# Four accumulators that were halves of two-bank tiles become one-bank tiles, with a new order list

## The chip, the cores and the metric

The kernel runs on one core of one Trainium2 chip. The metric is the device time of one execution in microseconds (us). The engines are TensorE (PE, with its weight loads as PEld), VectorE (DVE), ScalarE (ACT), GpSimd (POOL) and SyncE (SP, which issues DMAs).

## What is computed

Attention with a soft cap, then a gated feed-forward block with a token mix, then a second block that ends in a square product. Cut to what matters:

```python
s = cap * tanh(q @ k.T / 8 / cap)                       # 4 batches, 12 heads, 448 tokens, 64 each
x = softmax(s) @ v                                      # to (4, 448, 768)
h = relu(x @ w_in); u, v = halves of h                  # 1024 columns
x = (u * (w_spatial @ layer_norm(v) + b_spatial)) @ w_out
theta = x @ w_theta
y = w_tok_r @ (x * cos(theta)) + w_tok_i @ (x * sin(theta))
u = x + y
out = u + relu(u @ w_ch)                                # (4, 448, 768) @ (768, 768): the last stage
```

## The kernel before

All data are fp32. TensorE multiplies in fp32r, and for fp32's precision each factor is split in a high part and a low part (a cast, then `difference` L407, the rest as fp32r), so that each term is three products (`three`, `products`, whose matmuls all bear line L404).

The program is a plan. Functions such as `run`, `copy_out`, `plus` and `finish` don't issue instructions but record operations, each with an engine, keys that it reads and writes, and a function that issues it. A table of numbers, `ORDER` (lines 47 to about 330), lists the operations of the whole kernel, some 3430, in the order in which they are issued; `Plan.run` goes through it. The plan asserts only that no operation stands ahead of one whose keys it needs. Each engine then runs its own instructions in that order, and waits between engines follow from the tiles that instructions read and write: an instruction that touches a tile waits for the earlier ones on other engines which touch the same tile, unless both only read.

The last stage computes `u @ w_ch` for two pairs of batches with seven sums of block products in place of eight (`pair(c0, t)`). `a` and `S` are the weights and sums of them (`split_a` L1989, S on L2001, L2006 and L2010), `x` the split activations (cast L2065, difference L407, sums t_f on L2097). A `run` adds nine matmuls, 128 rows by 448 columns each, into one PSUM bank: three pieces of the inner dimension by three products. The pieces of several runs are interleaved on TensorE. When a bank is full it is read by one of `copy_out` (ACT, L2148, `p<-f_ps`) or `plus` (DVE, L2152, `p<-f_ps,p`); from the sums p, `finish` makes the result (DVE L2162), turns it round by four transposes into another bank (PE L2172, `o_ps`), copies it (ACT) and stores it (SP). The last piece of each pair ends in `end_of` (L2207 to L2234).

Six banks serve in turn (`new_bank` over `BANKS`, line 1892 on). Two are tiles of one bank in the pool `ps_mm`. The other four are the halves, 512 columns each, of two tiles of 1024 columns in the pool `ps_s`, which before that held the attention's scores and the transposes `x_ps`. `open_bank` makes such a tile, `bank_of` cuts out the half:

```python
fin["s", k] = ps_s.tile([128, 1024], F32, tag="s", name="f_ps")
...
return (fin["mm"][key[1]] if key[0] == "mm" else fin["s", key[1]][:, 512 * key[2]:512 * key[2] + 512])[:, 0:S]
```

The plan has a key for each half, `("s", k, h)`; the tile is one.

Of the kernel before, what the change touches and what calls it, by code (L numbers as in the profile page):

```python
# [342 lines left out]
def attn_moe_moe2_kernel(ctx: ExitStack, tc: tile.TileContext, q, k, v, cap, w_in, w_sp, b_sp, w_out,  # L343
# [13 lines left out]
    plan = Plan()  # L357
# [1531 lines left out]
    def open_bank(k):  # L1889
        fin["s", k] = ps_s.tile([128, 1024], F32, tag="s", name="f_ps")  # L1890
# [9 lines left out]
    def bank_of(key):  # L1900
        return (fin["mm"][key[1]] if key[0] == "mm" else fin["s", key[1]][:, 512 * key[2]:512 * key[2] + 512])[:, 0:S]
# [449 lines left out]
```

## Time and profile before

| | |
|---|---|
| time, three runs | 762.16, 763.88, 765.02 us (median 763.88) |
| profiled execution | 763.6 us, of which the span from first to last instruction 761.8 |
| mean granted TensorE clock | 0.997 of full speed |
| busy in the span: PE, DVE, ACT, POOL | 743.9, 620.2, 476.0, 343.0 us |
| share of the chain that ended last: PE, DVE, ACT, POOL | 72, 5, 2, 1% |

A busy time is the sum of the instructions of an engine. The stages follow one another with some overlap: attention and the first block to about 460 us, theta and the token mix to about 668, the last stage from there (its first products from about 650 on). For a stage the question is what TensorE's next instruction waits for, which the waits, the chain and the timeline tell; for a matmul the start counts, since the next begins before the end that the profile models.

### The profile page before, as it was taken

How to read it: one execution, taken by the hardware profiler on the slowest of the kernel's cores; microseconds unless marked ns; L12 is line 12 of the kernel's file. 1: busy time of each engine (PE TensorE's matmuls, PEld its weight loads, DVE VectorE, ACT ScalarE, POOL GpSimd, SP SyncE). 2: the span in 40 equal slices, each digit the busy share in tenths (PEclk: the TensorE clock that was granted, in tenths of full speed). 3: DMA queues.
4: the chain of work that ended last, by engine and by line, in shares of the span. 5: the costliest groups of instructions: out<-in, count | busy, mean ns of one | idle time of the engine just before them, and what ended most of it. 6: DMA issues, size and time to landing. Idle time of an engine off the chain costs nothing.

```text
span 761.8 us, 11555 instructions
## 1 busy us (share of the span) xinstructions
PE 743.9 (98%) x3965; PEld 643.1 (84%) x3965; DVE 620.2 (81%) x992; ACT 476.0 (62%) x798; POOL 343.0 (45%) x464
## 2 busy tenths in 40 slices
PE   7999999999999999999999999999999999999997
PEld 4655678888888888887899999999999999888896
DVE  4969988798687978799987776899878877997865
ACT  4989878788779878896454644543514533553453
POOL 4889675544555465561100012232332422877650
PEclk9999999999999999999999999999999999999999
DMA  6677333242432541431343330011210000000135
GB/s 174 190 202 182 109 101 93 57 106 64 101 93 51 123 98 33 119 76 43 92 144 115 121 94 1 1 43 43 62 42 22 22 2 1 1 0 1 37 108 147
DMA packets 82062, 59.31 MB, mean 78 GB/s; under 512 B 47330, under 2 KB 75204, under 8 KB 82004
## 3 DMA queue, kind: packets, MB, share of 16 engines
q1 hardware_dynamic: 80100, 54.61, 27.1%
q0 software_dynamic: 1152, 3.64, 1.5%
q8 instruction: 31, 0.51, 0.3%
q10 hardware_dynamic: 752, 0.33, 0.2%
q14 instruction: 27, 0.22, 0.1%
HBM read 44.18 MB, written 5.62 MB: 65 GB/s over the span
## 4 chain that ended last, share of the span: by engine, by line
PE 72%; DVE 5%; ACT 2%; POOL 1%; issue 1%; DVEq 0%; POOLq 0%; ACTq 0%
PE ps_mm L404 16%; PE y_ps L404 12%; PE th_ps L404 12%; PE f_ps L404 10%; PE acc L404 7%; PE sc L404 5%; PE ps_sum L404 3%; PE ps_av L404 3%; PE o_ps L2172 1%; PE tqk L711 1%; PE x_ps L1624 1%; DVE ll L407 1%; DVE p L2152 1%; DVE s L995 1%; PE tok_ps L1500 1%
## 5 line engine op out<-in xcount | busy, mean ns | idle before, releaser
L404 PE MATMUL y_ps<-tok_h,zt 128*128 128x448 f32 x312 | 99.0, 368 | 0.1
L824 ACT ACTIVATE e<-e,cap_sb 128x896 f32<-128x896 f32 x72 | 74.8, 1043 | 1.0
L821 ACT ACTIVATE e<-sc,icap 128x896 f32<-128x896 f32 x72 | 72.1, 1005 | 4.7 <-PE sc L404 3.8
L407 DVE TENSOR_TENSOR ll<-e,hh 128x896 fp32r<-128x896 f32 x54 | 59.3, 1103 | 16.0 <-ACT hh L829 14.1
L404 PEld LDWEIGHTS y_ps<-tok_h,zt 128*128 128x128 f32 x312 | 58.6, 188 | 5.1 <-POOL zt L407 0.4
L404 PE MATMUL th_ps<-th_ah,x 128*128 128x256 f32 x288 | 57.4, 284 | 0.0
L404 PE MATMUL y_ps<-tok_l,zt 128*128 128x448 f32 x156 | 57.4, 368 | 0.0
L407 POOL TENSOR_TENSOR zt<-z,zt 128x1024 fp32r<-128x1024 f32 x12 | 29.6, 2470 | 59.2 <-ACT zt L1739 59.2
L407 POOL TENSOR_TENSOR x<-x,x 128x384 fp32r<-128x384 f32 (+1 forms) x15 | 18.5, 1242 | 74.0 <-ACT x L1565 65.1
L404 PE MATMUL f_ps<-x,S 128*128 128x448 f32 x216 | 49.8, 372 | 1.6 <-DVE p L2152 1.0
L1678 POOL TENSOR_SCALAR n<-n 128x512 f32<-128x512 f32 (+1 forms) x24 | 16.0, 669 | 76.8 <-DVE n L1675 76.8
L404 PE MATMUL ps_mm<-w_in_h,x 128*128 128x512 f32 (+1 forms) x132 | 47.8, 400 | 0.9 <-DVE gated L1256 0.8
L404 PE MATMUL ps_mm<-x,w_in_h 128*128 128x448 f32 x168 | 48.3, 368 | 0.0
L404 PEld LDWEIGHTS th_ps<-th_ah,x 128*128 128x128 f32 x288 | 46.8, 190 | 0.8
L404 PE MATMUL sc<-yl,XH 128*128 128x448 f32 x126 | 46.4, 368 | 0.0
L404 PEld LDWEIGHTS f_ps<-x,S 128*128 128x128 f32 x216 | 39.6, 188 | 6.3 <-DVE p L2152 1.6
L404 PE MATMUL f_ps<-x,a 128*128 128x448 f32 (+2 forms) x171 | 38.8, 362 | 2.3 <-DVE p L2152 1.7
L404 PE MATMUL acc<-ll,vh 128*128 128x448 f32 x108 | 40.1, 371 | 0.8 <-DVE ll L407 0.8
L1739 ACT CAST zt<-z 128x1024 fp32r<-128x1024 f32 (+2 forms) x36 | 24.3, 691 | 26.2 <-DVE z L1710 22.7
L404 PE MATMUL th_ps<-th_al,x 128*128 128x256 f32 x144 | 40.6, 282 | 0.0
L450 ACT ACTIVATE hb<-bits 128x384 f32<-128x384 f32 (+4 forms) x40 | 22.7, 567 | 27.6 <-DMA bits<-in_moe_w_ch_dram 15.5
L404 PE MATMUL acc<-hh,vh 128*128 128x448 f32 x108 | 39.6, 367 | 0.0
(328 smaller groups left out, 2366.1 us busy)
## 6 DMA issues: line engine op xcount, KB each, us to landing
y<-y SPq DMA_DIRECT2D x60, 112.0 KB, 2.2
bits<-in_moe_w_ch_dram SPq DMA_DIRECT2D x12, 384.0 KB, 3.1
out_dram<-o SPq DMA_DIRECT2D x23, 192.0 KB, 2.4
rq<-in_q_dram SPq DMA_DIRECT2D x33, 128.0 KB, 2.7
rk<-in_k_dram SPq DMA_DIRECT2D x11, 384.0 KB
r<-d SPq DMA_DIRECT2D x16, 224.0 KB, 3.8
rv<-in_v_dram SPq DMA_DIRECT2D x18, 192.0 KB, 2.6
w_in_bits<-in_moe_w_in_dram POOLq DMA_DIRECT2D x6, 512.0 KB, 4.6
```

The source lines that it names most:

```text
L404: nc.tensor.matmul(out=ps, lhsT=a, rhs=r, start=(first and i == 0), stop=(last and i == len(terms) - 1))
L407: (engine or nc.vector).tensor_tensor(out=o, in0=x, in1=f32(hi), op=ALU.subtract)
L450: nc.scalar.activation(out=hb(), in_=f32(words()[:, :, 1]), func=ACTF.Copy, scale=2.0 ** -112)
L711: nc.tensor.transpose(o, a, ident)
L821: nc.scalar.activation(out=st["e", g], in_=src, func=ACTF.Tanh, scale=icap)
L824: nc.scalar.activation(out=st["e", g], in_=st["e", g], func=ACTF.Exp, scale=cap_sb)
L995: nc.vector.reciprocal(out=st["s"], in_=st["s"])
L1500: nc.tensor.transpose(o, a[:, kk * 128:(kk + 1) * 128], ident[0:n, 0:n])
L1624: nc.tensor.transpose(o, x2(b, m)[:, p * 128:p * 128 + 128], ident)
L1678: nc.gpsimd.tensor_scalar(out=sd["n"], in0=sd["n"], scalar1=1.0, scalar2=-MAGIC, op0=ALU.mult, op1=ALU.add)
L1739: nc.scalar.copy(out=o, in_=a)
L2152: op("dve", t + 0.2, 0.54, lambda: TT(out=fin["p", o], in0=bank_of(kb), in1=fin["p", j], op=ALU.add), r=[kb, ("p", j)], w=[("p", o)])
```

## The change

The pool `ps_s` goes to the right side of PSUM and gets a stack of its own, which one new operation `open_banks` closes when the last stage opens; in its place the operation opens the pool `ps_f` with four tiles of one bank each. `bank_of` takes these tiles. That is one operation less than before, and `ORDER` is another list over the whole kernel. Each engine has the same instructions in the same numbers; line numbers after the first edit move by 1, and by 3 from the last stage on (L2148 becomes L2151, L2152 becomes L2155).

```diff
 ORDER = [
-    9, 10, 38, 4, 7, 8, 12, 5, 36, 0, 6, 11, 35, 2, 31, 33, 37, 13, 14, 15, 29, 17, 16, 24, 30, 27, 32, 23, 18, 22, 34,
...
-    ps_s = Slots(plan, ctx.enter_context(tc.tile_pool(name="ps_s", bufs=1, space=PSUM)), 2)
     ps_1 = ctx.enter_context(tc.tile_pool(name="ps_1", bufs=1, space=PSUM))
     ps_mm = Slots(plan, ctx.enter_context(tc.tile_pool(name="ps_mm", bufs=1, space=PSUM)), 2)
+    ps_stack = ctx.enter_context(ExitStack())
+    ps_s = Slots(plan, ps_stack.enter_context(tc.tile_pool(name="ps_s", bufs=1, space=PSUM, side="right")), 2)
...
-    def open_bank(k):
-        fin["s", k] = ps_s.tile([128, 1024], F32, tag="s", name="f_ps")
+    def open_banks():
+        ps_stack.close()
+        ps_f = ctx.enter_context(tc.tile_pool(name="ps_f", bufs=1, space=PSUM, side="right", reuse_waits="tile"))
+        for k in range(2):
+            for h in range(2):
+                fin["s", k, h] = ps_f.tile([128, 512], F32, tag="f%d%d" % (k, h), name="f_ps")
 
     op("none", t - 4.0, 0.0, open_mm, w=[("mm", 0), ("mm", 1)])
     BANKS = [("mm", 0), ("mm", 1)]
-    for _ in range(2):
-        sk = ring("s", 2)[1]
-        halves = [("s", sk, h) for h in range(2)]
-        op("none", t0 - 2.0, 0.0, lambda sk=sk: open_bank(sk), w=[("s", sk)] + halves)
-        BANKS += halves
+    for sk in range(2):
+        BANKS += [("s", sk, h) for h in range(2)]
+    op("none", t0 - 2.0, 0.0, open_banks, w=[("s", 0), ("s", 1)] + BANKS[2:])
 
     def bank_of(key):
-        return (fin["mm"][key[1]] if key[0] == "mm" else fin["s", key[1]][:, 512 * key[2]:512 * key[2] + 512])[:, 0:S]
+        return (fin["mm"][key[1]] if key[0] == "mm" else fin[key])[:, 0:S]
```

In the rows of the order, a row is an instruction (or as many alike as `x3` says), with its line, what it writes and reads, and the engines whose semaphores it waits on. Before, `f_ps_7044` and `f_ps_7192` are the two tiles of two banks, `f_ps_7050` and `f_ps_7051` those of `ps_mm`. TensorE at the start of the last stage, at about 667.7 to 671.5 us of the trace of before:

```order
L404 MATMUL f_ps_7192<-x_6997,a_7138 128x448 [waits PE_49,Activation_49]
L404 MATMUL f_ps_7192<-x_6997,a_7138 128x448
L404 MATMUL f_ps_7192<-x_6997,a_7138 128x448 [waits DVE_49]
L404 MATMUL f_ps_7044<-x_6997,a_7138 128x448 x3
L404 MATMUL f_ps_7044<-x_7042,a_7152 128x448 [waits Activation_49]
L404 MATMUL f_ps_7044<-x_7042,a_7152 128x448
L404 MATMUL f_ps_7044<-x_7042,a_7152 128x448 [waits Pool_49]
L404 MATMUL f_ps_7192<-x_6997,a_7138 128x448 x3
```

The three products into `f_ps_7044` of row 4 go into its second half; row 5 goes on in that same half and waits for ScalarE, which reads the first half. After, the tiles of one bank are `f_ps_7096` to `f_ps_7099`, those of `ps_mm` are `f_ps_7076` and `f_ps_7077`. The same place on TensorE:

```order
L405 MATMUL f_ps_7099<-x_6997,a_7127 128x448 [waits PE_49]
L405 MATMUL f_ps_7099<-x_6997,a_7127 128x448 x2
L405 MATMUL f_ps_7098<-x_6997,a_7127 128x448 x3
L405 MATMUL f_ps_7098<-x_7044,a_7143 128x448 [waits Activation_49]
L405 MATMUL f_ps_7098<-x_7044,a_7143 128x448
L405 MATMUL f_ps_7098<-x_7044,a_7143 128x448 [waits Pool_49]
L405 MATMUL f_ps_7097<-x_7044,a_7143 128x448 x3
L405 MATMUL f_ps_7098<-x_7010,a_7081 128x448 x2
L405 MATMUL f_ps_7098<-x_7010,a_7081 128x448 [waits DVE_49]
```

The wait for ScalarE in row 4 is now one for an operand, as ScalarE's read is of `f_ps_7096` and no row here touches that. The second place is TensorE before at about 697.5 to 703 us, with two stops, at 699.65 (row 4) and 701.85 (row 8):

```order
L404 MATMUL f_ps_7192<-x_7042,a_7225 128x448 [waits DVE_49]
L404 MATMUL f_ps_7192<-x_7042,a_7225 128x448 x2
L404 MATMUL f_ps_7192<-x_7010,a_7225 128x448 x3
L404 MATMUL f_ps_7192<-x_7164,a_7405 128x448 [waits DVE_49]
L404 MATMUL f_ps_7192<-x_7164,a_7405 128x448 x2
L404 MATMUL f_ps_7192<-x_7169,S_6979 128x448 x2
L404 MATMUL f_ps_7192<-x_7169,S_6985 128x448
L404 MATMUL f_ps_7192<-x_7204,S_6982 128x448 [waits DVE_49]
L404 MATMUL f_ps_7192<-x_7204,S_6982 128x448
```

All rows are of one tile, of which VectorE reads one half while TensorE writes the other. The same place after:

```order
L405 MATMUL f_ps_7098<-x_7044,a_7237 128x448 [waits DVE_49]
L405 MATMUL f_ps_7098<-x_7044,a_7237 128x448 x2
L405 MATMUL f_ps_7098<-x_7010,a_7237 128x448 x3
L405 MATMUL f_ps_7099<-x_7216,S_6979 128x448 [waits DVE_49]
L405 MATMUL f_ps_7099<-x_7216,S_6979 128x448
L405 MATMUL f_ps_7099<-x_7216,S_6985 128x448
L405 MATMUL f_ps_7098<-x_7168,a_7410 128x448 x3
L405 MATMUL f_ps_7099<-x_7213,S_6982 128x448 x2
```

Two tiles take turns here, and a wait for VectorE stands only ahead of a bank's first product.

## Rows read from the trace of the kernel before

**Rows 1.** The page: busy time of each engine, share of span, instructions.

```profile
PE 743.9 (98%) x3965; PEld 643.1 (84%) x3965; DVE 620.2 (81%) x992; ACT 476.0 (62%) x798; POOL 343.0 (45%) x464
```

**Rows 2.** By stage: window, us, busy of PE, PEld, DVE, ACT, POOL; clock, DMA, GB/s.

```profile
460.00:640.00 180.00, 180.00 (x1219) 171.77 (x1219) 148.39 (x282) 77.35 (x150) 54.81 (x44) 1.00 0.09 25
...
664.00:690.00 26.00, 24.76 (x119) 21.92 (x118) 23.61 (x29) 12.53 (x28) 20.68 (x16) 1.00 0.00 0
690.00:720.00 30.00, 27.85 (x138) 24.35 (x137) 24.02 (x38) 12.52 (x30) 19.58 (x15) 1.00 0.09 24
720.00:750.00 30.00, 29.88 (x175) 26.82 (x173) 20.99 (x31) 14.52 (x40) 14.03 (x11) 1.00 0.40 107
```

**Rows 3.** Chain of waits from 664 us on: start us, us, what.

```profile
669.14 0.02 issue
669.16 0.54 ACT p L2148
669.70 0.04 issue
669.75 11.41 PE f_ps L404 x54
...
698.97 0.64 DVE p L2152
```

**Rows 4.** Waits of TensorE, 640 to 762 us: for what; total, times, longest.

```profile
PE f_ps L404 <- DVE p L2152: 2.7, 5, 0.7
PE f_ps L404 <- ACT p L2148: 1.2, 2, 0.6
PE o_ps L2222 <- DVE x L2209: 0.6, 2, 0.3
```

**Rows 5.** Timeline of TensorE: start us, us, instruction, count [idle before, releaser].

```profile
667.73 1.40 PE L404 MATMUL f_ps<-x,a 128*128 128x448 f32 x6
669.75 1.49 PE L404 MATMUL f_ps<-x,a 128*128 128x448 f32 x6 [0.62 <-ACT p L2148]
...
697.46 1.48 PE L404 MATMUL f_ps<-x,a 128*128 128x448 f32 x6
699.65 0.88 PE L404 MATMUL f_ps<-x,a 128*128 128x448 f32 x3 [0.72 <-DVE p L2152]
...
720.25 4.11 PE L404 MATMUL f_ps<-x,S 128*128 128x448 f32 x18
...
750.16 1.49 PE L404 MATMUL f_ps<-x,S 128*128 128x448 f32 x6 [0.28 <-DVE p L2152]
...
754.81 0.97 PE L404 MATMUL f_ps<-x,a 128*128 128x256 f32 x6 [0.28 <-DVE p L2152]
```

**Rows 6.** Groups of the page: busy us, mean ns, then idle before.

```profile
L404 PE MATMUL f_ps<-x,S 128*128 128x448 f32 x216 | 49.8, 372 | 1.6 <-DVE p L2152 1.0
```

**Rows 7.** Waits of TensorE's weight loads, 640 to 762 us.

```profile
PEld f_ps L404 <- DVE p L2152: 4.6, 6, 1.1
PEld f_ps L404 <- ACT p L2148: 2.4, 3, 1.0
...
PEld y_ps L404 <- POOL zt L407: 0.4, 1, 0.4
```

**Rows 8.** Timeline of VectorE in the same stretch.

```profile
649.98 0.61 DVE L407 TENSOR_TENSOR x<-x,x 128x448 fp32r<-128x448 f32 x1
...
659.63 0.41 DVE L1710 TENSOR_TENSOR z<-z,x_ps 128x256 f32<-128x256 f32 x1
...
680.21 1.57 DVE L407 TENSOR_TENSOR x<-t_f,x 128x448 fp32r<-128x448 f32 x1
...
698.97 1.16 DVE L2152 TENSOR_TENSOR p<-f_ps,p 128x448 f32<-128x448 f32 x2 [0.96 <-PE f_ps L404]
...
754.13 0.62 DVE L2152 TENSOR_TENSOR p<-f_ps,p 128x448 f32<-128x448 f32 x1 [1.47 <-PE f_ps L404]
```

**Rows 9.** Waits of TensorE, 60 to 340 and 340 to 640 us: the largest of each.

```profile
PE w_sp_ps L1096 <- DVE w_sp_l L407: 1.1, 2, 0.6
...
PE ps_mm L404 <- DVE gated L1256: 0.8, 1, 0.8
```

**Rows 10.** By stage again: the ten us after the w_sp waits.

```profile
80.00:90.00 10.00, 9.38 (x35) 7.54 (x36) 9.71 (x14) 7.76 (x12) 5.58 (x7) 0.83 0.43 129
```

341 rows, old and new, of the table ORDER are left out of this document.

## The prediction

> **What bounds the kernel now.** I read the page first: TensorE is busy in 743.9 of 761.8 us, the next engine, VectorE, in 620.2 [rows 1]. So the end can only move by what TensorE stands still, and the whole kernel holds less than 20 us of that. Then the busy time by stage [rows 2]: in 460 to 640 us TensorE has no gap (180.00 of 180.00), in the last stage it has: 24.76 of 26.00, 27.85 of 30.00, 29.88 of 30.00. The reader is to see beside it that VectorE stands at 23.61 of 26.00 us in the first of these stretches, nearly full too; that comes back as a rival.
>
> What the gaps are is told by the chain of waits [rows 3]. It goes matmul, then a read of 0.54 to 0.64 us on ScalarE or VectorE, then matmul. At 669.16 the copy L2148 begins 0.02 us after the matmuls before it, and the matmuls go on 0.05 us after it ends: both engines stand waiting for each other, with nothing queued between. The order of the kernel before shows why: PE writes three products into a bank, ACT or DVE reads the other half of the same two-bank tile, and PE goes on with the fourth product into the same bank as before. The reader waits for TensorE's three, which it does not read, and TensorE waits for the reader, whose half it does not write. Both are tied by the tile's name alone.
>
> TensorE's waits from 640 us on [rows 4] are all of this sort but the last two at the very end: DVE p five times, 2.7 us, ACT p twice, 1.2 us. The timeline of TensorE shows them one by one [rows 5]: 669.75, 699.65, 750.16 and 754.81 stand there; 681.76 (0.62), 701.85 (0.72) and 712.12 (0.71) read like the first two. Two more leave no gap in the row but stretch it: 697.46 and one inside the run that begins at 720.25. That makes nine.
>
> **The change, part by part.** *The stops.* A matmul's row lasts 0.37 us (mean 372 ns, [rows 6]) but the next one begins sooner: six take 1.40 us at 667.73 [rows 5], so the pitch is (1.40 - 0.37) / 5 = 0.206 us. The idle time of a row counts from the end of the 0.37, so each gap hides a further 0.37 - 0.21 = 0.16 us; and the six after a stop take 1.49 instead of 1.40, another 0.09. Seven stops with a gap: 2.7 + 1.2 = 3.9 us of idle time [rows 4], 7 x 0.16 = 1.1, 7 x 0.09 = 0.6, together 5.6 us. The stop at 697.46 adds some 0.2 (1.48 for six, and a start 0.14 late), the one in the run at 720.25 as much (4.11 us for 18, where 17 x 0.206 + 0.37 makes 3.87). Sum: **6.0 us**, all of it on TensorE, which the chain follows. By the idle column alone it would be 3.9.
>
> Idle and loss part here because matmuls overlap. The Trainium skill (Perfetto Trace Analysis, Identifying the Most-Contended Engine) says that matmul busy time is a bad measure, since pipelined matmuls look otherwise in the trace than they cost; it names the share of weight loads as the better one. The weight loads' waits for the same readers are 4.6 + 2.4 = 7.0 us [rows 7]; the sum by these would give 763.6 - 7.0 + 0.5 = 757.1, by the idle column 760.2. I keep the sum by starts.
>
> *Does the edit remove all nine?* In the kernel after each bank is a tile, so a read waits for the writes of its own bank. What is left is true reuse: by the order of after at least 15 matmuls (15 x 0.206 = 3.1 us) stand between the last product into a bank and the first of its next use, where before five stops had none at all. The read in between takes 0.64 us [rows 3]. It has 2.4 us to spare, more than any one instruction of VectorE that I saw in its way (1.57 us, [rows 8]). So these waits go to nothing, at most to a few tenths if two slow VectorE instructions fall together.
>
> *What is late next.* TensorE then asks earlier for its operands, by up to 6 us at the end. They are splits on VectorE and GpSimd (L407) and the pieces S. The same 128x448 split takes 0.61 us at 649.98 and 1.57 at 680.21, with GpSimd busy beside it [rows 8], so one operand can come 0.96 us later than another of its kind. Before, such waits appear only under other matmuls, 0.4 us for zt [rows 7]. Bounds: 0 where the new order keeps the distance, 1.0 where one slow split is met on the path. I take **0.5 us**, in the middle, since 0.4 is the only such row. At the end of the stage the gain passes on: VectorE waits 1.47 us for TensorE at 754.13 [rows 8], so nothing of the tail stands on VectorE.
>
> *Closing the pool and opening a new one* issues no instruction: counts on every engine are the same. But the new pool's tiles take the place of the old one's, so their first writes wait until those were read. The last user of these tiles is x_ps, transposes that VectorE reads for the last time at 659.63 [rows 8]; the first product into that place comes at 667.73 [rows 5], 7.7 us after the read ends, and the other tile was free before. The new order brings x_ps 12 matmuls earlier, which widens this. Price nothing; if the cover were gone, one wait of at most the read's 0.41 us.
>
> *The rest of the order.* The list was made anew over the whole kernel, so all engines' rows shift by a few places, with the same operations and durations. From 460 to 640 us there is nothing to win [rows 2]. From 60 to 460 us TensorE's waits are few and short: w_sp 1.1 us, gated 0.8 [rows 9], nine groups and 4.6 us in all to 640 us. A new order can take half of these away or breed as many. There is a costlier kind of row: after the two w_sp waits of 79.08 and 80.39 the granted clock is 0.83 in the ten us from 80 on [rows 10], at 1.2 GHz for part of it, where 0.17 x 10 = 1.7 us of full-speed time is missing. If that stretch is met once more or once less the time moves by about 2.5. I take **0**, with -2.5 to +2.5 as bounds.
>
> Sum against the profiled execution: 763.6 - 6.0 + 0.5 + 0 = **758.1 us**, 0.7% less. The profiled execution lies 0.3 us under the median of 763.88, so no correction is made.
>
> **The rivals.** *A: the stop goes, the next engine is late.* For it: VectorE is busy in 23.61 of 26.00 us from 664 to 690 [rows 2]; without the two stops there (1.7 us) that stretch would be 24.3 us, and VectorE 97% full, with no room for an order that is not perfect. Against: it falls to 24.02 of 30.00 in the next stretch, and part of its time is waiting for the very same stops (0.96 us at 698.97, [rows 8]). Price: the 1.7 us are not won, and three slow splits more at 0.96 are met, 2.9: 763.6 - 6.0 + 1.7 + 2.9 = 762.2 us.
>
> *B: slower, by waits in the attention stage.* The new order starts late there one more operand of TensorE at several places, as w_sp now, and after each the clock falls: 1.1 us of waiting [rows 9] and 1.7 us of clock [rows 10] are 2.8 us a place. Two places leave 758.1 + 5.6 = 763.7, so from there on it decides; three make 766.5, four 769.3. For it: from 60 to 90 us VectorE is full, so an operand moved back a place is late by its whole duration. Against: only one such place exists in 400 us of the present order, and the moves are of a few rows.
>
> *C: the stops stay.* There are six banks before and six after, and if the banks were too few the wait would only take another name. The Trainium skill (Perfetto Trace Analysis, Optimization Strategy) holds that the same gap coming again and again can mean too little PSUM for the next tile, which by that rule would leave 763.6. The rows speak against it: TensorE stops within a bank, after three of its nine products, where no new bank is asked for, and the reader begins 0.02 us after TensorE's last [rows 3].
>
> **How the numbers follow.** The forecast has 0.68: nine stops counted one by one, each with its cause in the order. A 0.14 (762.2), B 0.12 (of this 0.06 for 766 to 767 and 0.06 beyond), C 0.06 (763.6). The likeliest gives 758.1. Its own range is 755.1 (no operand waits, 2.5 won in the rest) to 761.1 (1.0 of operand waits, 2.5 lost). To hold 8 in 10 it must take in A: 755.0 to 762.8. A measurement of this kernel can tell about 0.5% from no change, that is 760.1 and 767.7. Faster than 760.1: most of the forecast, 0.62, and nothing else, though the bound of +2.5 in the rest is wide, so I add 0.05 for a rest that gains: 0.67. Slower than 767.7: 0.06, the end of B. Between: 0.27.
>
> **What would show it.** Right: in the profile after, TensorE's waits from 640 us on have no row with p as releaser, or under 0.5 us of them; its busy share from 664 to 720 us is over 97%; runs of f_ps matmuls go on at 0.206 us a piece through each read; VectorE's rows of p no longer begin 0.02 us after a TensorE row. Six us less from 664 us to the end, and the time at which the last theta matmul is done unchanged within 2.5 us. Wrong by A: TensorE waits for x, S or t_f in that stage, with VectorE over 95% busy. Wrong by B: the theta stage begins later than before by 5 us or more, and rows of clock under 0.9 stand in the attention stage. Wrong by C: rows with p as releaser stay at 3 us or more.

## The result

The kernel after takes **753.19 us** (median of 4 runs, 751.25 to 753.88) against 764.13 for the kernel before (4 runs, 762.16 to 765.02): ratio 0.9856, 95% interval 0.9829 to 0.9883, 10.9 us less. The forecast was 758.1 with 755.0 to 762.8, so the direction was right and the size was not: the gain is nearly twice the one forecast, and lies under the range. The profiled execution took 752.78 us, 10.8 less than that of before.

The page of after, against [rows 1]:

```profile
PE 739.3 (98%) x3965; PEld 643.6 (86%) x3965; DVE 610.0 (81%) x992; ACT 475.3 (63%) x798; POOL 353.0 (47%) x464
```

TensorE's busy share is 98% as before, although 10.8 us are gone. The Trainium skill (Perfetto Trace Analysis, Identifying the Most-Contended Engine) says that this share is no good measure of how close TensorE is to its peak, and names that of the weight loads among the better ones; here the trace agrees, it went from 84 to 86%. So the time was sought by the starts of instructions that both kernels have. Two marks serve for all kernels of this study: the transposes of rk that follow the w_sp transposes, near 90 us, and the first matmul of theta, near 450 us. TensorE's timeline at these two places, and at the transposes of rk before them (start us, us, instruction), before:

```profile
70.56 0.49 PE L711 MATMUL tqk<-ident,rk 128*128 128x128 f32 x3
...
90.68 0.49 PE L711 MATMUL tqk<-ident,rk 128*128 128x128 f32 x3
...
449.45 0.28 PE L404 MATMUL th_ps<-th_ah,x 128*128 128x256 f32 x1
```

and after:

```profile
68.79 0.49 PE L712 MATMUL tqk<-ident,rk 128*128 128x128 f32 x3
...
85.89 0.49 PE L712 MATMUL tqk<-ident,rk 128*128 128x128 f32 x3
...
444.54 0.28 PE L405 MATMUL th_ps<-th_ah,x 128*128 128x256 f32 x1
```

From these and the spans, 761.8 and 751.0: the first stretch lasts 90.7 and 85.9 us, the second 358.8 and 358.7, the third 312.4 and 306.5. So 4.8 us were won before 91 us, 0.1 in the middle, and 5.9 from theta to the end. Of the 4.8 us, 1.8 are won by the transposes of rk near 70 us, and 3.0 between these and the first mark.

In the last stage the waits of TensorE from 636 us on, against [rows 4], have p no longer (waited for: us in total, times, longest):

```profile
PE o_ps L2225 <- ACT o L2229: 0.6, 1, 0.6
PE f_ps L405 <- DVE S L2013: 0.3, 1, 0.3
```

and the timeline, against [rows 5], shows one run of products through all reads:

```profile
662.50 3.88 PE L405 MATMUL f_ps<-x,a 128*128 128x448 f32 x18
...
671.78 9.46 PE L405 MATMUL f_ps<-x,S 128*128 128x448 f32 x45
...
687.12 1.68 PE L405 MATMUL f_ps<-x,S 128*128 128x448 f32 x7 [0.31 <-DVE S L2013]
```

Five banks' worth, 45 matmuls, take 9.46 us, and 44 pitches of 0.206 us and one of 0.37 make 9.43: nothing stands between. The only wait in a product is for an operand, S. The stages' busy times, against [rows 2] (window, us, busy of PE, PEld, DVE, ACT, POOL, clock, DMA, GB/s; the stage begins some 5 us earlier here):

```profile
659.00:685.00 26.00, 26.00 (x131) 23.76 (x130) 25.55 (x30) 14.09 (x32) 23.61 (x18) 1.00 0.00 1
685.00:715.00 30.00, 29.58 (x144) 26.39 (x144) 29.55 (x42) 12.37 (x28) 19.83 (x16) 1.00 0.09 23
715.00:745.00 30.00, 30.00 (x190) 27.89 (x189) 18.87 (x30) 15.22 (x44) 12.96 (x10) 1.00 0.50 135
```

VectorE is now at 98% for 56 us, and keeps up.

### The profile page after: what moved, and what is told of

Same layout as the page of the kernel before. It is cut to its first block, busy times and chain, and to the rows that moved or that the text cites. A ratio compares the mean times of both kernels' runs of the same rounds, so it can differ in the third digit from the quotient of the medians.

```text
span 751.0 us, 11570 instructions
## 1 busy us (share of the span) xinstructions
PE 739.3 (98%) x3965; PEld 643.6 (86%) x3965; DVE 610.0 (81%) x992; ACT 475.3 (63%) x798; POOL 353.0 (47%) x464
## 4 chain that ended last, share of the span: by engine, by line
PE 82%; DVE 9%; DMA 3%; ACT 2%; issue 1%; SPq 1%; POOL 1%; DVEq 0%; POOLq 0%; ACTq 0%
PE ps_mm L405 18%; PE y_ps L405 12%; PE th_ps L405 12%; PE acc L405 11%; PE f_ps L405 10%; PE sc L405 7%; PE ps_sum L405 3%; PE ps_av L405 3%; DVE ll L408 2%; PE tqk L712 2%; DMA w_in_bits<-in_moe_w_in_dram 2%; PE o_ps L2175 1%; PE x_ps L1625 1%; DVE x L408 1%; DVE s L996 1%
## 5 line engine op out<-in xcount | busy, mean ns | idle before, releaser
L405 PE MATMUL acc<-hh,vl 128*64 128x448 f32 x108 | 39.6, 367 | 0.0
L1740 ACT CAST zt<-z 128x1024 fp32r<-128x1024 f32 (+2 forms) x36 | 24.3, 690 | 23.4 <-DVE z L1711 19.9
```

The costliest lines, as they stand in the source:

```text
L405: nc.tensor.matmul(out=ps, lhsT=a, rhs=r, start=(first and i == 0), stop=(last and i == len(terms) - 1))
L1740: nc.scalar.copy(out=o, in_=a)
```

## The experiments

Each was timed beside the kernel before on the same chip, in four sets on four chips, so times of different sets are compared by their ratios to before. Microseconds won or lost are worked out from the ratios. The kernel before scatters: its runs beside these experiments go from 759.4 to 768.0 us, and its median per set of runs from 762.8 to 765.4; a ratio within 0.2% of 1 is read as no difference. The marks of all profiled executions stand in a table behind the experiments.

**The two parts of the change, one at a time.** e1_banks has the tiles and leaves the old list untouched. Each two-bank tile has a pool of its own there, so that the two `open_bank` operations can stay where they are:

```diff
     def open_bank(k):
-        fin["s", k] = ps_s.tile([128, 1024], F32, tag="s", name="f_ps")
+        ps_stacks[k].close()
+        ps_f = ctx.enter_context(tc.tile_pool(name="ps_f%d" % k, bufs=1, space=PSUM, side=PS_SIDES[k], reuse_waits="tile"))
+        for h in range(2):
+            fin["s", k, h] = ps_f.tile([128, 512], F32, tag="f%d%d" % (k, h), name="f_ps")
```

> The kernel before with its own order list, to the last row, in which each of the two-bank tiles of the last stage is replaced by two tiles of one bank. Theory: the nine stops cost 6.0 us and are gone by the tiles alone, with about 0.4 us of new operand waits: 5.6 us less than before, ratio 0.9927, and no wait of TensorE for p in the last stage. Rival: the last stage needs the new order as well, since in the old one some banks are asked for again 9 matmuls after their last product; then less than 3 us are won and waits for p stay.

Measured: 760.54 us, ratio 0.9951 (0.9933 to 0.9969), 3.7 us less. Waits of TensorE from 636 us on:

```profile
PE o_ps L2189 <- DVE x L2179: 0.8, 1, 0.8
PE o_ps L2239 <- ACT o L2243: 0.6, 1, 0.6
```

No matmul waits for p any more (the weight loads have one such wait of 0.4 us, under other matmuls), so the tiles alone take all nine stops away, and the rival, in which such waits stay, falls. The size is short of the theory's 5.6 us: by the time it is 3.7 (2.4 to 5.1), and in the traces theta to the end lasts 308.2 us instead of 312.4, 4.2 less. Of what is missing one row names a part: the transposes wait 0.8 us for x on VectorE.

e2_order has the new list and halves of two-bank tiles:

```diff
         for k in range(2):
-            for h in range(2):
-                fin["s", k, h] = ps_f.tile([128, 512], F32, tag="f%d%d" % (k, h), name="f_ps")
+            fin["s", k] = ps_f.tile([128, 1024], F32, tag="f%d" % k, name="f_ps")
```

> The kernel after, with the new order list, in which the four banks are halves of two-bank tiles again. Theory: what was won ahead of the last stage (5.5 us by the two traces) comes from the order alone and stays; in the last stage two stops of 0.87 us with no matmul between and one of 0.5 come back, and a few with 6 or 7 matmuls between may show: 2.3 to 4 us of the 5.6 are lost, so 7 to 9 us less than before, ratio 0.988 to 0.991. Rival: the gain ahead of the last stage hangs on the new pool; then the ratio is 0.995 or more.

Measured: 757.35 us, ratio 0.9915 (0.9890 to 0.9939), 6.5 us less. The same view:

```profile
PE f_ps L405 <- DVE p L2154: 1.9, 4, 0.7
PE f_ps L405 <- ACT p L2150: 1.2, 3, 0.8
PE o_ps L2224 <- DVE x L2211: 0.6, 2, 0.3
```

The theory's range of the ratio lies in the interval, and the rival falls, though more stops came back than the three that were counted: seven, 3.1 us of idle time where before had 3.9. Theta to the end lasts 310.1 us, 3.6 more than in after. So the order alone wins more than the tiles alone, and most of it is not in the last stage, where its trace has 2.3 us of it. e1 and e2 together, 3.7 + 6.5, make 10.2 of the 10.9.

**Where the order's gain lies.** The list was cut behind its first 573 entries, which hold the first 100 us of TensorE's work. e5_first takes these from after, the rest of the list and the tiles from before; e6_rest is the counterpart.

> The kernel before, in which the first 573 entries of the list (the first 100 us of TensorE's work, up to about 128 us) stand as in after, and the rest in the order of before, with the two-bank tiles. Theory: some 4 us of what the order alone won (7 us) lie in these entries, since the traces of the three kernels with the old order lose 24 to 29 us there and the two with the new one 23 to 25: ratio 0.995. Rival: what differs there between traces is chance in when the loads land, and the gain of the order lies behind it: ratio 0.999 or more.

> The kernel after, with its one-bank tiles, in which the first 573 entries of the list stand in the order of before. Theory: it lacks what e5_first wins, about 4 us, and has the rest of the 11: 757 us, ratio 0.991. Rival: nothing hangs on the first 573 entries; then it is as fast as after, ratio 0.986.

Measured: e5_first 761.95 us, ratio 0.9958 (0.9944 to 0.9972), 3.2 less; e6_rest 757.94 us, ratio 0.9908 (0.9889 to 0.9928), by the ratios 4 us over the kernel after. Both hold the theory: 3 to 4 us hang on the first 573 entries and are independent of the tiles. In e6_rest theta to the end lasts 306.3 us, as in after; its first mark stands at 90.6 us, as in before.

**What in these entries.** Each of the following changes the kernel before at one point of its first 100 us. e3_start reorders the first issues of SyncE's queue, and with them the first load of rq:

```diff
 first issues of SyncE, by number of the operation
-38 (tt), 8 (rq), 5 (rq), 36 (tt), 0 (cap), 6 (rq), 35, 31, 33, 37, 13, 32, 34
+5 (rq), 0 (cap), 36 (tt), 6 (rq), 38 (tt), 8 (rq), 31, 33, 35, 13, 34, 32, 37
```

> The kernel before, in which only the first 13 issues of SyncE's queue stand in the order of after: the load of rq that TensorE's first transposes need goes first, not fourth. Theory: TensorE's wait of 1.56 us at 5.4 us goes and 1.75 us stay won to the end, ratio 0.9977. Rival: the next wait (XT from GpSimd at 10.6 us, then the exponentials) takes it up and nothing is won, ratio 1.000.

Measured: 764.49 us, ratio 0.9996 (0.9970 to 1.0022): nothing. Its profiled execution, 760.36 us, is one of the quickest of its twelve; by itself it would have told of a gain of 3 us, and its trace can't show where the usual execution loses it. Two later traces with the same 13 issues, e10 and e12, show one way: the first transposes of rk start at 7.3 and 7.4 us, 8.9 before, but the next ones at 15.9 and 16.0, 15.2 before, since TensorE waits 1.7 and 1.8 us there for a load of tt. SyncE's second issue of tt<-in_q_dram comes at 10.6 us in the new order, at 6.7 in the old one. In e3's own quick execution that wait is 0.2 us.

e4_wsp takes the w_sp waits of [rows 9], with the fall of the clock behind them [rows 10]:

```diff
 TensorE's operations at 71 to 81 us (sum: four acc matmuls)
-sum(360), w_sp(380), w_sp(383), av(357), sum(364), w_sp(386), w_sp(389)
+w_sp(383), w_sp(380), av(357), sum(360), w_sp(386), sum(364), w_sp(389)
```

> The kernel before, in which only six operations of TensorE around the w_sp transposes at 71 to 81 us stand in the order of after (the last two w_sp transposes have a group of four acc matmuls between them, which stood ahead of both). Theory: the two waits for w_sp_l (1.1 us idle) go, and with them the stretch of 3.2 us at half the clock right after, 1.7 us: 3.2 us in all, ratio 0.9958, clock 1.00 from 80 to 90 us. Rival: VectorE is what is late there, the waits only move and the clock falls as before: under 1 us, ratio 0.999 or more.

Measured: 765.10 us, ratio 1.0012 (0.9993 to 1.0030): nothing, by its rival. TensorE's timeline in e4 there:

```profile
76.65 0.75 PE L1096 MATMUL w_sp_ps<-ident,w_sp_p 128*128 128x128 f32 x4 [1.55 <-DVE w_sp_l L407]
```

The two waits of 0.55 became one of 1.55 us, and the clock falls as before, only earlier: it is 0.90 from 70 to 80 us and 0.93 from 80 to 90. So the wait for w_sp_l was moved, not taken away: in this trace VectorE is what is late.

e7_sp gives SyncE's queue alone the new order, e8_compute the four engines alone.

> The kernel before, in which SyncE's queue alone (it issues most loads) has the order of after in the first 69 issues, 34 of which have moved; all other engines keep the order of before. Theory: the first 100 us are bound by loads, and the order of the issues is what made them robust: 3 to 4 us less, ratio 0.995 to 0.996. Rival: the engines' own order counts; ratio 0.999 to 1.000.

> The kernel before, in which TensorE, VectorE, ScalarE and GpSimd have the order of after in their first instructions (the same 573 entries) and SyncE's queue keeps the order of before. Theory of the loads: nothing, ratio 0.999 to 1.000. Rival, by the engines' order: 3 to 4 us less, ratio 0.995 to 0.996. If both this and e7_sp win little, it takes both together.

Measured: e7_sp 769.54 us, ratio 1.0074 (1.0051 to 1.0096), 5.7 us **slower**; e8_compute 763.91 us, ratio 0.9985 (0.9971 to 0.9999), 1.1 us less. SyncE's order alone loses, and that of the four engines alone wins no more than is read as no difference: it takes both together, as the last sentence for e8 had it. Where e7_sp loses time, its waits from 30 to 90 us show, SyncE's first, then TensorE's:

```profile
SPq L987 <- DVE c L983: 10.0, 2, 8.3
...
PE sc L404 <- DMA y<-y: 3.1, 1, 3.1
```

SyncE's new order has the move of the inverted sums (`spread`, L987) earlier, and VectorE's old order makes these (`invert`, c) as late as ever; SyncE stands there for 8.3 us and issues nothing from 45.9 to 54.3 us of the trace; the move of y for TensorE's next scores, behind it in the queue, is issued at 56.2, and TensorE waits 3.1 us for y. In e5_first, with both orders, the wait for c is 2.3 us.

e9_w_in takes up a like wait in the trace of before, where SyncE stands 3.4 us for VectorE (w_in_f) ahead of a load of w_in, with y behind it. It moves that one issue behind y and Y:

```diff
 SyncE's issues around 46 us
-w_in(105), w_in(119), y(304), rk(471), Y(345), v(288)
+w_in(105), y(304), rk(471), Y(345), w_in(119), v(288)
```

> The kernel before, in which one issue of SyncE's queue stands three places later: the load of w_in that waits for VectorE (3.4 us at 46.7 us in the trace of before) goes behind the loads of y, rk and Y instead of ahead of them. Theory: that wait holds up the y that TensorE needs next, and is what the new order takes away in the first 100 us; 2 to 3 us less, ratio 0.996 to 0.9975, and no run of the slower sort (763 us and more), which is most of those of before. Rival: TensorE is as late for another reason; ratio 0.999 or more.

> As e9_w_in, and the first 13 issues of SyncE in the order of after as well (e3_start). Theory: with the wait gone the 1.5 to 1.8 us of the start are no longer taken up by it, so this wins what e5_first did or more: 3.5 to 4.5 us, ratio 0.994 to 0.9955. Rival: the start is taken up by something else too; then it is as e9_w_in.

> The kernel after, in which that load of w_in goes back directly behind the load of w_in before it, ahead of two small moves of sums (d2 and d) as in the kernel before. Theory: SyncE waits for VectorE again and y with it: 1.5 to 3 us of the gain are lost, ratio to before 0.988 to 0.990. Rival: in the new order VectorE frees that buffer in time; as after, 0.986.

> The kernel before with three things done by hand in its old list: the one-bank tiles of e1_banks, the first 13 issues of e3_start and the moved load of e9_w_in. Theory: the parts add, 3.8 us and 3.5 to 4.5: 7.3 to 8.3 us less, ratio 0.989 to 0.9905; what is left to after (some 3 us) is the rest of the order. Rival: they overlap, ratio over 0.992.

Measured: e9_w_in 763.87 us, ratio 1.0007 (0.9987 to 1.0028); e10_w_in_start 762.87 us, 0.9993 (0.9971 to 1.0015); e11_after_w_in 753.49 us, 0.9873 (0.9848 to 0.9898); e12_by_hand 759.96 us, 0.9962 (0.9940 to 0.9984). The theory falls in e9, e10 and e12: SyncE's wait goes (the first row is of before, the second of e9, both from 30 to 62 us) and the time does not move, and tiles, start and w_in together win no more than the tiles alone. The interval of e11 holds its theory and its rival; put back into the kernel after (ahead of one small move, d, which is all that stood between), where SyncE then waits 2.9 us for w_in_f instead of 0.2, the load costs nothing that can be told (753.19 us in after).

```profile
SPq L1038 <- DVE w_in_f L468: 3.9, 2, 3.4
...
SPq L1038 <- DVE w_in_f L468: 0.7, 2, 0.5
```

The last three ask which part of SyncE's order the engines' order needs.

> As e8_compute (the four engines in the order of after in their first instructions), and SyncE's first 13 issues in the order of after too; the rest of its queue as before. Theory: the start's 1.5 us are worth something only where the engines behind it take them up, so this wins what e5_first won, 3.2 us, ratio 0.996. Rival: the later issues, up to the 69th, are the ones that count; then as e8_compute, 0.9985.

> As e8_compute, and SyncE's issues 14 to 69 in the order of after; its first 13 as before. The counterpart of e13_engines_start: by the theory of the start as e8_compute, 0.9985 to 1.000; by its rival 0.996 to 0.997. If both lie between, the two parts share the gain.

> As e7_sp (SyncE's first 69 issues in the order of after), and VectorE's first instructions in that order as well; TensorE, ScalarE and GpSimd as before. Theory: e7_sp lost 5.7 us since SyncE stood 8.3 us at an issue whose data (c) VectorE made late, with a load of y for TensorE behind it; with VectorE's order that makes c earlier the loss goes and the gain of e5_first appears: ratio 0.996 to 0.998. Rival: the other engines have a part in it, ratio 1.000 or more.

Measured: e13_engines_start 761.75 us, ratio 0.9988 (0.9968 to 1.0009); e14_engines_later 763.16 us, 1.0017 (0.9993 to 1.0041); e15_sp_vector 767.32 us, 1.0051 (1.0026 to 1.0076). The kernel before had its lowest median in this set, 762.82. e13 wins at most little, e14 nothing; the start may be the half that counts, but that is not settled. By its time e15 goes to its rival. In its trace, though, the first half of its theory came true (the first row is of 30 to 90 us, the second of the first 30 us):

```profile
SPq L987 <- DVE c L983: 1.8, 1, 1.8
...
PE tqk L695 <- DMA tt<-in_q_dram: 1.8, 1, 1.8
```

The wait for c is 1.8 us where e7 had 8.3, TensorE does not wait for y, and from the transposes of rk near 50 us to those near 70 it takes 21.1 us, as before (20.9; e7 25.3). The loss is in a new place, the start: TensorE waits 1.8 us for tt and 1.7 for rq, its granted clock is 0.50 from 15 to 20 us, and the transposes of rk that start at 24.4 us before start at 27.8. The times bear this out: the five of its twelve runs with a mean clock under 0.996 take 768.5 to 769.4 us, the four with 0.999 or more 763.9 to 765.9. So VectorE's order mends the one stop of e7. Why the loads at the start are late here and not in e7 (23.7 us at that mark), which has the same issues, is not shown; and no run of e15 has the gain of e5, which has the other engines' order too.

The marks of the profiled executions, from TensorE's timelines: first mark; from there to the first theta matmul; from there to the end of the span (us).

| kernel | first 573 entries | last stage | to the first mark | to theta | to the end |
|---|---|---|---|---|---|
| before | old | old, halves | 90.7 | 358.8 | 312.4 |
| after | new | new, tiles | 85.9 | 358.7 | 306.5 |
| e1_banks | old | old, tiles | 92.2 | 359.0 | 308.2 |
| e2_order | new | new, halves | 88.3 | 357.5 | 310.1 |
| e5_first | new | old, halves | 87.5 | 360.1 | 313.2 |
| e6_rest | old | new, tiles | 90.6 | 359.1 | 306.3 |
| e3, e4, e8 to e10, e13, e14 | in part | old, halves | 87.0 to 91.3 | 359.3 to 361.0 | 312.0 to 313.5 |
| e7_sp, e15 | in part | old, halves | 94.5, 92.4 | 359.0, 361.1 | 313.2, 313.2 |
| e12_by_hand | in part | old, tiles | 91.5 | 358.9 | 307.9 |
| e11_after_w_in | new but for one | new, tiles | 87.0 | 358.2 | 306.4 |

The last column is as good as one number for each kind of last stage: 312.0 to 313.5, 308, 310, 306.4; within the first kind, the five traces from 313.2 on have one more wait for p and one for x, 0.4 and 0.6 us. The first column scatters by five us between executions of much the same instructions. Its three traces of the old order lie at 90.6 to 92.2, the three of the new at 85.9 to 88.3: 4 us on average. A single trace can't carry this (e3 has 87.0 and no gain in time); the times of e5 and e6 do.

By the ratios the tiles win 3.7 us and the first 573 entries 3.2 to 4, by the traces the new order of the last stage 1.7 more. That is 8.6 to 9.4 of the 10.9; the rest is no larger than these intervals, and no run names it.

## Why the prediction was wrong in size

*The stops* were right as a cause: e1 shows that with the tiles no matmul waits for p. Their size was not: they were put at 6.0 us by the starts, 3.9 by the idle column, 7.0 by the weight loads, and at 5.5 net of new operand waits; the tiles alone give 4.2 by the traces with the old order (e1) and 3.6 with the new one (e2 against after), nearer to the idle columns, 3.9 and 3.1. From theta to the end 5.9 us went, because the new order of that stage gives 1.7 more, which the sum did not have; that 5.9 lies so near 5.5 is in part luck. The new order also spares waits for operands (0.8 us for x in e1); what else took the difference from the tiles is not shown. The operand wait that I took for 0.5 us is one row of 0.3 for S.

*What is late next*, rival A: VectorE is nearly full, as that rival had it, and still in time. In 26 us it is busy in 25.55, and only one product waits.

*The rest of the order* is the step that failed. It was put at 0 with bounds of 2.5 us, worked out from TensorE's waits from 60 to 640 us, 4.6 us in all. The first 60 us, in which TensorE waits 5.3 us, were left out of the sum without a reason. What the runs show in place of 0 is 3.2 us (e5) to 4 us (e6 against after) for the first 573 entries. With that term at 3 to 4 the sum would have been 754 to 755. From the first mark to theta 0 was right, 358.8 and 358.7 us. The sign that told of the miss was the last theta matmul, which was to be unchanged within 2.5 us: it starts at 636.98 us, 642.47 before.

In the two traces 1.8 of the 4.8 us are won by 70 us, and 3.0 from there to the first mark, in the stretch of the two w_sp waits, which the prediction had in its rows: met once less, it was to bring about 2.5. In the trace of after TensorE does not wait for w_sp_l, and the stretch lasts 17.1 us for 20.1. But e2, which has the same list, waits 1.4 us there, with VectorE waiting 0.9 and 0.7 us for moves of sums just ahead, and takes 19.9. So these 3.0 us are not shown to come from the list.

*Why the first 573 entries win* is not settled. Shown is that SyncE's queue and the engines need each other's order (e5 against e7, e8 and e15), and one way in which they hurt each other when they differ (e7: one issue waits for VectorE, and the y behind it is late; in the trace of e15, with VectorE's order, that is gone). Not shown is which waits of the old order make up the 3 to 4 us: the load that held up SyncE and the late first load of rq were taken away without a gain in time, and the w_sp wait was only moved, so it is not tested.

*Rival B* had the place right, the attention stage's start, and the sign wrong. Its price of the clock, 1.7 us, was too high. Eight traces have the two w_sp waits; in four (before, e1, e7, e12) the granted clock is then 0.83 from 80 to 90 us, in the other four (e3, e6, e9, e10) it stays at 1.00. From the transposes of rk near 70 us to those near 90 the first four take 19.8 to 20.1 us, the others 19.2 to 19.6: in these traces the fall costs 0.6 us on average, and it does not follow each time. *Rival C* fell with e1.

## What to carry over

A tile that holds two accumulators ties their writers and readers together by its name: look for an engine that stops in the middle of an accumulation for a reader of something else. The sum of such stops by starts (6.0 us) is what TensorE loses at them; what comes back can be less (4.2 here), since the next waits take a part. Where a change brings a new order of the whole program, give every stretch of it a term, above all the first, where single traces differed most here. The order of SyncE's queue was good only together with the order of the engines that it waits for.

## What was not expected

The scatter between traces has a place. The kernel before ran in 759.4 to 768.0 us. It was profiled once, but the traces of its near relatives point to the first 90 us: the first mark of kernels with the old entries, or most of them, lies anywhere from 87.0 to 92.2 us; from there to theta the traces with the old last stage lie within 2.3 us, and from theta on the eleven of them agree to 1.5 us in 312.
